# Attention with RMS-normed queries and keys, then a GELU feed-forward: in the second attention, batch 2's first loads are issued ahead of the transposes of batch 1's last heads

## The chip, the cores and the metric

The kernel runs on one core of a Trainium2 chip. That core has five engines with a queue of instructions each: TensorE (PE; its weight loads are shown apart, as PEld), VectorE (DVE), ScalarE (ACT), GpSimd (POOL) and SyncE (SP), which here only issues DMAs. Each engine works through its own queue in order and waits for the others by semaphores. Sixteen DMA engines move the data.

The metric is the device time of one execution in microseconds (us). The kernel before takes 390.83 us, the median of three executions (390.56 to 392.31).

## The reference

Eight batches of twelve heads, 448 tokens and 64 channels go through an attention whose queries and keys are normed by their root mean square and scaled by a gain per channel. The result, taken as 3584 tokens of 768 channels, goes through two matrix products with a GELU between them.

```python
def _attn_ref(q, k, v, g_q, g_k):            # q, k, v: (8, 12, 448, 64)
    def rmsnorm(x, g):
        rms = np.sqrt(np.mean(x * x, axis=-1, keepdims=True) + 1e-06)
        return x / rms * g
    q_n, k_n = (rmsnorm(q, g_q), rmsnorm(k, g_k))
    scores = 1.0 / np.sqrt(q.shape[-1]) * np.matmul(q_n, k_n.transpose(0, 1, 3, 2))
    scores = scores - np.max(scores, axis=-1, keepdims=True)
    attn = np.exp(scores)
    attn = attn / (np.sum(attn, axis=-1, keepdims=True) + 1e-09)
    return np.matmul(attn, v)

def _moe_ref(x, w_in, w_out):                # (3584, 768) x (768, 2048) x (2048, 768)
    h = x @ w_in
    c = np.float32(np.sqrt(2.0 / np.pi))
    g = 0.5 * h * (1.0 + np.tanh(c * (h + 0.044715 * h * h * h)))
    return g @ w_out
```

## The kernel before

**Tiling.** A batch's twelve heads are three chunks of four heads, numbered c = 0, 1, 2. For each chunk the queries and the keys are loaded as one tile each (`rawq`, `rawk`, 128 partitions x 896 numbers, 448 KB), squared, summed per row and channel group (`total`, L173), turned into reciprocal roots, multiplied by them (`normed`, L278, tiles `nrmq` and `nrmk`), and transposed so that the channels lie on the partitions (`qT`, `kT`). The gains of queries and keys are one product per channel, and it is multiplied into `kT` only: where the transpose is made by TensorE, that happens as VectorE copies the result out of PSUM (`put`, L305); where the transpose is made by a DMA (`dma_trans`, L319), VectorE multiplies the finished `kT` in place afterwards (`gain`, L325).

**Stages.** The program is a chain of stages, one batch after another: the attention of batch b + 1 is run together with the second matrix product of the feed-forward for tokens that are done (L495), and then comes the first matrix product for batch b + 1 (L537). The transposes, loads and sums for the next batches are strewn among them. What the change touches lies in the second attention, that of batch 1, for which `attention(1, ...)` is called with b = 0 in the loop of L918. In the trace of before it runs from 50.8 to 76.7 us.

**The order of the work is written out by hand.** `SECOND` (L577) holds two rows for this attention. The first is TensorE's: `u` is one unit of scores (four matmuls of L335; unit n belongs to chunk n // 7, so u14 is the first unit of chunk 2), `s` the row sums of a chunk and `x` its product with the values (both L387), and `8r` is eight steps of the second matrix product (four matmuls each). The second is VectorE's: `A`, `B`, `F`, `G` are additions of exponentials (L355 to L362), `T` (L397), `R` (L402) and `S` (L409) make the reciprocals of the row sums, and `M` (L422) writes the attention's output `xT`:

```python
"A0 L0 B0 F0 G0 L1 T0 R0 K0 S0 a0 M0 a1 T1 a2 R1 a3 S1 A2 a4 B2 a5 F2 M1 T2 R2 S2 M2"
```

`L0`, `L1`, `K0` and `a0` to `a5` are slots: what stands for them in the list `extra` is emitted at that place, and `"first"` in `extra` is emitted ahead of the whole attention. ScalarE makes one exponential (L343) for each unit and copies finished tiles of the second product out of PSUM (L518), from which SyncE stores them (L456).

**Loads and transposes in this stage.** `late_loads(b, c)` sets one number of each new raw tile to zero on VectorE (L142) and then issues the load on SyncE's queue; the load therefore waits for that place in VectorE's queue. `late_transposed(1, 2)` does the same for the transposes of chunk 2: VectorE sets one number of `qT` and one of `kT` (L908), and SyncE issues the two DMA transposes behind them (L319). `gpsimd_waits(x)` (L793) makes GpSimd copy one number of x, so that what follows on GpSimd waits for whoever writes x. In slot `K0` GpSimd is told to square batch 2's chunks 0 and 1 (L164): two whole tiles for chunk 0, four halves for chunk 1. VectorE sums them in `a0` to `a5`.

**Where things stand before the change.** The transposes of chunk 2 of batch 1 are emitted in step 6 of the first product for batch 0, before the attention begins. The loads of batch 2 come in `L0` (chunk 0), `L1` (chunk 1) and `a1` (chunk 2). The gain of chunk 2 comes in `K0`, behind the reciprocal R0, and GpSimd's squares wait for that gain.

Of the kernel before, what the change touches and what calls it, by code (L numbers as in the profile page):

```python
# [17 lines left out]
def kernel(  # L18
# [11 lines left out]
    nc = tc.nc  # L30
# [81 lines left out]
    kT = consts.tile([128, NCH, NT, 2, R], BF16)  # L112
# [5 lines left out]
    def load(b, c, n, parts=1, engs=(nc.sync,)):  # L118
        t = rawqk.tile([P, 2, NT, D], F32, tag=f"raw{n}", name=f"raw{n}")
        src = {"q": q, "k": k}[n]  # L120
        raws[n, b, c] = t
        m = 2 // parts
        return [
            lambda i=i: engs[i].dma_start(
                t[:, i * m:(i + 1) * m].rearrange("p a t d -> p a (t d)"),
                src[b, 4 * c + 2 * i * m:4 * c + 2 * (i + 1) * m].rearrange(
                    "(a r) (p t) d -> (r p) a (t d)", r=2, t=NT
                ),
            )
            for i in range(parts)  # L130
        ]
# [6 lines left out]
    def late_loads(b, c):  # L138

        for n in "qk":  # L140
            for go in load(b, c, n):
                nc.vector.memset(raws[n, b, c][:1, 0, 0, :1], 0.0)  # L142
                go()
# [140 lines left out]
    def qT_of(b):  # L284
        if b not in qT:
            qT[b] = qkp.tile([128, NCH, NT, 2, R], BF16, tag="qT", name="qT")
        return qT[b]
# [3 lines left out]
    def turn(b, c, n, ts=slice(0, NT)):  # L291

        if ts.start == 0 and ts.stop == NT:
            tps[n] = ps_m.tile([128, 1024], BF16, tag="mm", name="tp")
        for t in range(ts.start, ts.stop):
            nc.tensor.transpose(  # L296
                tps[n][:, t * 128:(t + 1) * 128],
                nrms[n, b, c][:, t].rearrange("p a d -> p (a d)"), ident,
            )

    def put(b, c, n, ts=slice(0, NT), eng=nc.vector):
        dst = (kT if n == "k" else qT_of(b))[:, c, ts]
        src = tps[n][:, :TR].rearrange("p (t r s) -> p t r s", r=2, s=R)[:, ts]
        if n == "k":
            nc.vector.tensor_scalar(dst, src, gcol[:, 0:1], None, op0=ALU.mult)  # L305
        elif eng is nc.scalar:
            nc.scalar.copy(dst, src)
        else:
            nc.vector.tensor_copy(dst, src)

    def trans(b, c, eng=nc.vector):
        for n in "qk":
            turn(b, c, n)
            put(b, c, n, eng=eng)
# [9 lines left out]
    def gain(b, c):  # L324
        nc.vector.tensor_scalar(kT[:, c], kT[:, c], gcol[:, 0:1], None, op0=ALU.mult)  # L325

    exs, ess, oas, scs = {}, {}, {}, {}
# [463 lines left out]
    def gpsimd_waits(x):  # L791

        nc.gpsimd.tensor_copy(mark, x)  # L793
# [106 lines left out]
    def transposed(b, c):  # L900
        for n in "qk":
            dma_trans(b, c, n)

    def late_transposed(b, c):

        for n in "qk":
            dst = kT if n == "k" else qT_of(b)
            nc.vector.memset(dst[:1, c, 0, 0, :1], 0.0)  # L908
        transposed(b, c)
# [4 lines left out]
    def normed_both(b, c, eng):  # L914
        for n in "qk":
            normed(b, c, n, eng)

    for b in range(B):  # L918
        m1, side, extra, ends = [], [], [], []
        if b == 0:  # L920

            m1 = [(0, lambda: total(1, 0, "k"),
                   lambda: total(1, 2, "q"), lambda: total(1, 2, "k"),
                   lambda: rsqrt_newton(1), lambda: normed_both(1, 2, nc.gpsimd),
                   lambda: normed(1, 0, "k", nc.gpsimd)),
                  (2, lambda: total(1, 1, "q"), lambda: total(1, 1, "k"),
                   lambda: normed(1, 0, "q", nc.vector), lambda: rsqrt_last(1),
                   lambda: normed_both(1, 1, nc.vector)),
                  (6, lambda: trans(1, 0, nc.scalar), lambda: late_transposed(1, 2)),
                  (7, lambda: trans(1, 1))]  # L930
            extra += [("L0", lambda: late_loads(2, 0)), ("L1", lambda: late_loads(2, 1)),
                      ("a1", lambda: late_loads(2, 2)),
                      ("K0", lambda: gain(1, 2))]

            for n in "qk":
                sqs[n, 2, 1] = [
                    nrmp.tile([P, NT, 2, D], BF16, tag=f"nrm{m}", name="sq")
                    .rearrange("p t a d -> p (t a d)").bitcast(F32)
                    .rearrange("p (a t d) -> p a t d", a=1, t=NT) for m in "qk"
                ]  # L940

            extra.append(("K0", lambda: gpsimd_waits(kT[:1, 2, 0, 0, :1])))
            at = 0
            for c in range(2):
                for n in "qk":
                    for hs in (slice(0, 1), slice(1, 2)) if c else (both,):
                        extra += [
                            ("K0", lambda c=c, n=n, hs=hs: square(2, c, n, nc.gpsimd, hs)),
                            (f"a{at}", lambda c=c, n=n, hs=hs: total(2, c, n, hs))]
                        at += 1  # L950
        elif b + 1 < B:

            m1.append((0, lambda: gpsimd_waits(ess[b, NCH - 1][:1, 0, 0, :1])))
            for c in range(NCH):
                if b == 1 and c + 1 == NCH:
                    m1 += [(0, lambda: total(2, 2, "q")), (0, lambda: total(2, 2, "k")),
                           (0, lambda: rsqrt_last(2))]
                m1 += [(0, lambda c=c: normed_both(b + 1, c, nc.gpsimd)),
                       (4 * c + 4, lambda c=c: transposed(b + 1, c))]
            m1 += [(9, lambda: gain(b + 1, 0)), (14, lambda: gain(b + 1, 1))]  # L960
        if 0 < b and b + 2 < B:
            m1 += [(4, lambda: loads(b + 2, 1)), (8, lambda: loads(b + 2, 2))]
            for c, at in ((0, 4), (1, 9)):
                for i, (n, a) in enumerate((n, a) for n in "qk" for a in range(2)):
                    m1.append((at + i, lambda c=c, n=n, a=a: squared(b + 2, c, n, a)))
                m1 += [(at + 2, lambda c=c: total(b + 2, c, "q")),
                       (at + 4, lambda c=c: total(b + 2, c, "k"))]
            for n in "qk":
                m1.append((13, lambda n=n: square(b + 2, 2, n, nc.gpsimd)))
                extra.append(("first", lambda n=n: total(b + 2, 2, n)))  # L970
        if 0 < b and b + 1 < B:
            extra.append(("first", lambda: gain(b + 1, 2)))
        m1 = plan(*m1)
        for f in range(nf // 2 if b == 0 else nf):
            i, part = f // 4 * 2, f % 4
            if b == 0:
                if f == 2:
                    mm1(0, 5)
                    square(1, 1, "k", nc.scalar)
                elif f > 2:  # L980
                    mm1_pair(f)
            elif f == 1:
                mm1_turn(b, 0, 1, late)
                mm1_turn(b, 1, 1, late)
                mm1_turn(b, 0, 0, late, end=True)
            elif f == 3:
                mm1_turn(b, 1, 0, late, end=True)
            elif part == 1:
                mm1_turn(b, i, 0, range(HP), begin=True)
                mm1_turn(b, i + 1, 0, range(HP), begin=True)  # L990
                mm1_turn(b, i, 1, range(HP), end=True)
            elif part == 3:
                mm1_turn(b, i + 1, 1, range(HP), end=True)
            for fn in m1.get(f, ()):
                fn()
        if b + 1 == B:
            final(b)
            break
        nc.scalar.preload_act_table_set(EXP_SET)
        if b + 2 < B:  # L1000
            ends.append(lambda: rsqrt(b + 2, slice(0, NCH if b else NCH - 1)))
            side += [(0 if b else 11, lambda: load_v(b + 2, 0, HP))]
            if b + 3 < B:
                side.append((3, lambda: loads(b + 3, 0)) if b else (14, lambda: late_loads(3, 0)))
        if b == 0:
            start.close()
            ps_x = ctx.enter_context(
                tc.tile_pool(name="ps_x", bufs=1, space=bass.MemoryType.PSUM))
            for i in (2, 3):
                rounds.append(ps_x.tile([128, 2, 512], F32, tag=f"t{i}", name=f"t{i}"))  # L1010
            late_on.append(b)
        attention(b + 1, plan(*side), plan(*extra), ends)
# [30 lines left out]
```

## Time and profile before

| | |
|---|---|
| median of three executions | 390.83 us (390.56 to 392.31) |
| the profiled execution | 391.29 us, of which the span of instructions is 389.5 us |
| mean granted TensorE clock | 0.998 |
| TensorE busy | 381.4 us, 98% of the span |
| ScalarE busy | 278.7 us, 72% |
| VectorE busy | 236.6 us, 61% |
| GpSimd busy | 125.2 us, 32% |

All times of a trace are in us from the start of the span. In a row of the timeline stand the start, the duration, the engine, the line of the kernel, the operation, what it writes and reads, shapes and the number of instructions; in brackets the idle time ahead of it and what ended it. In a row of a table by stages stand the stretch, its length, and for each engine its busy time and in brackets its instructions, then the granted clock, the mean busy share of the DMA engines and what they moved in GB/s. For a DMA, the "time to landing" runs from the start of its issue on the queue to the last part of its data.

### The profile page before, as it was taken

To read this page: it belongs to the slowest core of one execution; us is meant where nothing else is said; L and a number is where in the kernel's file an instruction comes from. 1 tells how busy PE (TensorE), PEld (TensorE's weight loads), DVE (VectorE), ACT (ScalarE), POOL (GpSimd) and SP (SyncE) were. 2 spreads that over 40 slices of the span, in tenths; PEclk is the share of its full clock that TensorE was granted. 3 is DMA by queue.
4 is the path that set the end of the run, shared out by engine and by line. 5 is a ranking of instruction groups with operands and counts; after the bars stand their busy time and mean duration, and the time that the engine had idled before them with its cause. 6 is when DMAs were issued, how large, how long until landed. Compare 5 with 4: busy or idle time off the path is not lost.

```text
span 389.5 us, 17541 instructions
## 1 busy us (share of the span) xinstructions
PE 381.4 (98%) x8060; PEld 293.4 (75%) x8060; DVE 236.6 (61%) x367; ACT 278.7 (72%) x353; POOL 125.2 (32%) x107
## 2 busy tenths in 40 slices
PE   8799999999999999999999999999999999999996
PEld 5465567877888788877888778877888778887664
DVE  5899938976597259835589256953598204980010
ACT  6995589767994689757996589946897449944300
POOL 4996505484005540083102740064400900000000
PEclk9999999999999999999999999999999999999999
DMA  8999997999614993379822995159622621120033
GB/s 276 315 224 210 210 163 250 247 266 256 114 44 94 223 222 71 84 133 221 185 69 65 197 239 108 44 104 253 112 74 54 123 46 42 44 65 4 2 82 81
DMA packets 64414, 54.68 MB, mean 140 GB/s; under 512 B 37588, under 2 KB 59988, under 8 KB 64340
## 3 DMA queue, kind: packets, MB, share of 16 engines
q1 hardware_dynamic: 53904, 41.33, 45.3%
q0 software_dynamic: 10128, 11.80, 18.5%
q8 instruction: 63, 1.03, 1.1%
q10 hardware_dynamic: 308, 0.43, 0.4%
q14 instruction: 11, 0.09, 0.1%
HBM read 45.61 MB, written 11.01 MB: 145 GB/s over the span
## 4 chain that ended last, share of the span: by engine, by line
PE 92%; ACT 4%; DMA 2%; POOL 1%; SPq 0%; DVE 0%; issue 0%; DVEq 0%
PE t L537 33%; PE t L495 32%; PE t L387 9%; PE t L335 7%; PE t L463 5%; PE t L556 4%; ACT ex L343 4%; DMA rawq<-in_q_dram 2%; POOL g L164 1%; PE h L436 1%; PE tp L296 0%; PE o L387 0%; SPq L745 0%; PE os L387 0%; DVE ss L173 0%; ACT lg L198 0%
## 5 line engine op out<-in xcount | busy, mean ns | idle before, releaser
L343 ACT ACTIVATE ex<-t,shift 128x896 bf16<-128x896 f32 x168 | 156.2, 1016 | 1.9 <-PE t L335 1.6
L495 PE MATMUL t<-wout,g 64*64 64x384 bf16 (+1 forms) x3456 | 150.6, 305 | 0.0
L537 PE MATMUL t<-xT,win 64*64 64x448 bf16 x2688 | 128.6, 349 | 0.0
L495 PEld LDWEIGHTS <-g 64*64 64x64 bf16 x3456 | 112.6, 107 | 19.5
L537 PEld LDWEIGHTS <-win 64*64 64x64 bf16 x2688 | 96.1, 107 | 31.0
L543 ACT ACTIVATE g<-t 128x896 bf16<-128x896 f32 x56 | 50.5, 915 | 57.1 <-PE t L537 57.1
L173 DVE TENSOR_REDUCE ss<-sq 128x14 f32<-128x896 f32 (+3 forms) x45 | 44.6, 997 | 52.9 <-ACT sq L162 49.1
L335 PE MATMUL t<-qT,kT 64*64 64x448 bf16 x672 | 58.1, 351 | 2.3 <-ACT ex L343 0.8
L355 DVE TENSOR_TENSOR es<-ex 128x1792 bf16<-128x1792 bf16 x20 | 21.1, 1058 | 32.4 <-ACT ex L343 32.4
L278 POOL TENSOR_TENSOR nrmq<-rawq,rinv 128x896 bf16<-128x896 f32 (+1 forms) x21 | 34.8, 1659 | 17.6 <-ACT rinv L205 9.9
L793 POOL COPY mark<-es 1x1 bf16<-1x1 bf16 x6 | 1.1, 177 | 117.1 <-DVE es L362 112.9
L278 POOL TENSOR_TENSOR nrmk<-rawk,rinv 128x896 bf16<-128x896 f32 x20 | 33.6, 1679 | 0.0
L387 PE MATMUL t<-ex,vb 64*64 64x448 bf16 x588 | 31.9, 350 | 0.0
L335 PEld LDWEIGHTS <-kT 64*64 64x64 bf16 x672 | 25.4, 106 | 8.3 <-DVE kT L305 2.2
L397 DVE STREAM_TRANSPOSE st<-t 128x448 f32<-128x448 f32 x42 | 24.7, 627 | 9.1 <-PE t L387 9.1
L387 PEld LDWEIGHTS <-vb 64*64 64x64 bf16 x672 | 23.5, 107 | 7.1 <-issue 0.8
L409 DVE STREAM_TRANSPOSE rb<-rc 128x896 f32<-128x896 f32 (+1 forms) x25 | 26.7, 1067 | 0.3
L701 DVE COPY osb<-t 128x384 f32<-128x384 f32 (+1 forms) x4 | 2.0, 508 | 35.2 <-PE t L463 35.2
L422 DVE TENSOR_TENSOR xT<-t,rb 128x896 bf16<-128x896 f32 x21 | 22.8, 1085 | 0.8
L513 ACT COPY osb<-t 128x768 f32<-128x768 f32 (+1 forms) x18 | 12.6, 701 | 14.0 <-PE t L495 14.0
L164 POOL TENSOR_TENSOR sq<-rawq 128x896 f32<-128x896 f32 (+1 forms) x9 | 13.6, 1511 | 27.9 <-DVE ss L173 21.6
L358 DVE TENSOR_TENSOR es<-es,ex 128x1792 bf16<-128x1792 bf16 x20 | 21.3, 1063 | 0.7 <-ACT ex L343 0.7
(103 smaller groups left out, 315.4 us busy)
## 6 DMA issues: line engine op xcount, KB each, us to landing
rawq<-in_q_dram SPq DMA_DIRECT2D x23, 448.0 KB, 5.1
rawk<-in_k_dram SPq DMA_DIRECT2D x23, 448.0 KB, 5.8
out_dram<-osb SPq DMA_DIRECT2D x42, 192.0 KB, 2.7
vb<-in_v_dram POOLq DMA_DIRECT2D x6, 672.0 KB, 7.4
win<-in_moe_w_in_dram POOLq DMA_DIRECT2D x8, 384.0 KB, 10.5
wout<-in_moe_w_out_dram POOLq DMA_DIRECT2D x3, 768.0 KB, 17.3
out_dram<-osb SPq DMA_DIRECT2D x24, 96.0 KB, 3.5
vb<-in_v_dram POOLq DMA_DIRECT2D x2, 448.0 KB, 15.7
```

The lines of the kernel that those rows point to most:

```text
L173: nc.vector.reduce_sum(sss[b][:, seat(b, c), "qk".index(n), hs, ts], squares(b, c, n, hs, ts), axis=AX.X)
L278: eng.tensor_mul(nrms[n, b, c][:, ts].rearrange("p t a d -> p a t d"), raws[n, b, c][:, :, ts], root[:, :, ts].to_broadcast([P, 2, m, D]),)
L335: nc.tensor.matmul(sc[r * R:(r + 1) * R, a, :S], kT[rs, c, t, r], qT[b][rs, c, :, r], start=True, stop=True,)
L343: nc.scalar.activation(exs[b, c][:, t], scs.pop((b, c, t))[:, :, :S], AF.Exp, scale=scale, bias=shift)
L358: nc.vector.tensor_add(es, es, ex[:, 4:6])
L387: nc.tensor.matmul(o[r][a * D:(a + 1) * D], vb[b % 2][rs, 2 * c + a, i] if what else ones[rs], es[i][rs, a], start=(i == 0), stop=(i == n ...
L397: nc.vector.transpose(st[:, r].rearrange("p a b -> p (a b)"), o[r])
L409: nc.vector.transpose(oas["rb"][:, rs].rearrange("p r s -> p (r s)"), rc.to_broadcast([128, (rs.stop - rs.start) * m, 32]),)
L422: nc.vector.tensor_mul(xT[b][:, 2 * c:2 * c + 2], oas["o", c, 1][:, :, :S], oas["rb"])
L495: mm = nc.tensor.matmul(o[a * R:(a + 1) * R, bank, :hi - lo], g[rs, f, at:at + R], wout[rs, f, lo:hi], start=(n == 0), stop=(n == len(step ...
L537: mm = nc.tensor.matmul(h[a * R:(a + 1) * R, j, :S], win[rs, c, at:at + R], xT[b][rs, c], start=begin and c == cs[0], stop=end and c == cs ...
L543: nc.scalar.activation(g[:, 2 * i:2 * i + 2, (b % 2) * S:(b % 2 + 1) * S], h[:, :, :S], AF.Gelu_apprx_tanh,)
```

## The change

Four entries of the plan of the second attention are moved or replaced:

- `late_transposed(1, 2)`, the two DMA transposes of batch 1's chunk 2 with their two VectorE memsets, goes from step 6 of the first product to slot `L0`, behind VectorE's first addition A0.
- `late_loads(2, 0)`, the first two loads of batch 2 with their memsets, goes from `L0` to `"first"`, ahead of the attention. On SyncE's queue these loads now stand ahead of the two transposes.
- `gain(1, 2)`, VectorE's multiplication of the transposed keys by the gain, goes from `K0` to `a1`, behind M0 and behind the memsets of the loads of batch 2's chunk 2.
- GpSimd's squares of batch 2 wait for the reciprocals of R0 (`oas["rc"]`) and no more for the gain.

```diff
@@ -926,11 +926,11 @@
                   (2, lambda: total(1, 1, "q"), lambda: total(1, 1, "k"),
                    lambda: normed(1, 0, "q", nc.vector), lambda: rsqrt_last(1),
                    lambda: normed_both(1, 1, nc.vector)),
-                  (6, lambda: trans(1, 0, nc.scalar), lambda: late_transposed(1, 2)),
+                  (6, lambda: trans(1, 0, nc.scalar)),
                   (7, lambda: trans(1, 1))]
-            extra += [("L0", lambda: late_loads(2, 0)), ("L1", lambda: late_loads(2, 1)),
-                      ("a1", lambda: late_loads(2, 2)),
-                      ("K0", lambda: gain(1, 2))]
+            extra += [("first", lambda: late_loads(2, 0)), ("L0", lambda: late_transposed(1, 2)),
+                      ("L1", lambda: late_loads(2, 1)), ("a1", lambda: late_loads(2, 2)),
+                      ("a1", lambda: gain(1, 2))]
@@ -939,7 +939,7 @@
-            extra.append(("K0", lambda: gpsimd_waits(kT[:1, 2, 0, 0, :1])))
+            extra.append(("K0", lambda: gpsimd_waits(oas["rc"][:1, :1])))
```

## The prediction

> **What bounds the kernel now.** I read the page first: TensorE's share, and the chain that ended last.
>
> ```profile
> PE 381.4 (98%) x8060; PEld 293.4 (75%) x8060; DVE 236.6 (61%) x367; ACT 278.7 (72%) x353; POOL 125.2 (32%) x107
> PE 92%; ACT 4%; DMA 2%; POOL 1%; SPq 0%; DVE 0%; issue 0%; DVEq 0%
> ```
>
> The second row is the chain: TensorE's own work sets the end. Next the busy times by stage: the second attention up to its unit u14, the rest of it, and all that follows to the last product.
>
> ```profile
> 50.84:65.52 14.68, 14.68 (x345) 10.54 (x348) 7.94 (x16) 14.65 (x18) 2.67 (x3) 1.00 1.12 214
> 65.52:76.71 11.19, 11.19 (x260) 8.89 (x253) 11.19 (x21) 9.16 (x15) 5.54 (x8) 1.00 0.88 221
> 76.71:346.77 270.06, 270.06 (x6462) 218.70 (x6457) 171.61 (x235) 208.25 (x257) 81.87 (x56) 1.00 0.62 129
> ```
>
> In each stretch TensorE (the first engine after the length) is busy for the whole length. Two things follow. The change can't win much, since no TensorE stall of any size is there to be removed. And a stall that it puts into TensorE's queue has no idle time behind it that could take it up. (Busy matmuls are modelled and may hide waits of some hundredths, so "much" means a few tenths here.) In the second stretch VectorE, the third figure, is busy for all 11.19 us too, so it has no room for extra work there either.
>
> So the question is which of TensorE's waits moves. One candidate: u14, the first unit that reads the chunk 2 keys whose transpose and gain are moved. The timelines of TensorE and its weight loads, and VectorE's, around it:
>
> ```profile
> 64.03 1.52 PE L387 MATMUL t<-ex,vb 64*64 64x448 bf16 x28
> 65.36 0.14 PEld L335 LDWEIGHTS <-kT 64*64 64x64 bf16 x4
> 65.52 0.39 PE L335 MATMUL t<-qT,kT 64*64 64x448 bf16 x4
> ```
>
> ```profile
> 62.19 0.33 DVE L402 RECIPROCAL rc<-st 128x28 f32<-128x28 f32 x1
> 62.43 0.35 DVE L325 TENSOR_SCALAR kT<-kT,gcols 128x896 bf16<-128x896 bf16 x1
> 62.70 1.10 DVE L409 STREAM_TRANSPOSE rb<-rc 128x896 f32<-128x896 f32 x1
> 64.69 1.09 DVE L173 TENSOR_REDUCE ss<-sq 128x14 f32<-128x896 f32 x1 [0.88 <-POOL sq L164]
> 65.69 1.08 DVE L422 TENSOR_TENSOR xT<-t,rb 128x896 bf16<-128x896 f32 x1
> 66.71 1.07 DVE L173 TENSOR_REDUCE ss<-sq 128x14 f32<-128x896 f32 x1
> 67.72 0.64 DVE L397 STREAM_TRANSPOSE st<-t 128x448 f32<-128x448 f32 x1
> ```
>
> Before, the gain (L325) is over at 62.78, and u14's weights load at 65.36 without a wait for it. M0 (L422) starts at 65.69, when x0, the product with the values, has ended (64.03 + 1.52 = 65.55).
>
> **The change part by part.**
>
> *The gain goes behind M0.* This is the term that decides. VectorE's queue now reads S0, a0, M0, the memsets, gain, sum, T1. M0 stays where x0's end puts it, and the next instruction starts at 66.71; the memsets of the loads cost nothing there, as they already stand between M0 and the sum that starts at 66.71. So the gain runs from 66.71. How long? The rows of all other gains give 443 to 875 ns, the one of this stage 353:
>
> ```profile
> L325 DVE TENSOR_SCALAR kT<-kT,gcols x18: 443/445/875, 88.9 to 314.7; 128x896 bf16<-128x896 bf16 x18
> 59.72 0.63 DVE L362 TENSOR_TENSOR es<-es,ex 128x896 bf16<-128x896 bf16 x1
> 60.49 0.36 PE L387 MATMUL t<-es,ones 64*64 64x448 bf16 x4
> ```
>
> I take 0.40, between the 0.35 and the median 0.445: it ends at 67.11. From the end of a VectorE result to the first matmul that waits for it the last two rows give 60.49 - 60.35 = 0.14. u14 thus starts at 67.25 in place of 65.52, **1.73 us later**. Behind u14 in TensorE's queue stands everything else: s1, u15 to u20, the second product, the whole rest of the program.
>
> What is late next? T1 needs s1, which needs u14's place in the queue: T1 comes 1.73 late by TensorE, but it was held back by the sum until 67.72 where s1 had ended by 67.4 or so, hence 1.45 late. From T1 on VectorE runs without a gap to F2, for which s2 waits:
>
> ```profile
> 68.87 0.57 DVE L173 TENSOR_REDUCE ss<-sq 128x7 f32<-128x448 f32 x1
> 74.12 0.60 DVE L360 TENSOR_TENSOR es<-es 128x896 bf16<-128x896 bf16 x1
> 74.81 0.39 PE L387 MATMUL t<-es,ones 64*64 64x448 bf16 x4
> 66.51 6.62 ACT L343 ACTIVATE ex<-t,shift 128x896 bf16<-128x896 f32 x7
> ```
>
> F2 ends at 74.72 + 1.45 = 76.17, and s2, at 74.81 + 1.73 = 76.54, finds it done. The seven exponentials of chunk 2 shift with their units and stay ahead of the additions. So no second stall here: +1.73.
>
> *The gain leaves the place ahead of S0.* S0 starts 0.27 earlier (62.70 - 62.43), and nothing gains by it: M0 waits for x0, not for S0. 0.
>
> *GpSimd waits for the reciprocals.* They are there at 62.52, the gain at 62.78. The squares start some 0.26 earlier than these rows:
>
> ```profile
> 62.85 0.18 POOL L793 COPY mark<-kT 1x1 bf16<-1x1 bf16 x1 [17.52 <-DVE kT L325]
> 66.26 0.92 POOL L164 TENSOR_TENSOR sq<-rawq 128x448 f32<-128x448 f32 x1
> ```
>
> The first sum, a0, comes 0.26 earlier into the gap before M0: 0. But the gain and the squares may now run side by side, which the old wait excluded (rivals).
>
> *The loads of batch 2's chunk 0 go ahead.* Their memsets come behind VectorE's last copy before the attention, some 5.4 us before 57.1:
>
> ```profile
> 51.03 0.68 DVE L305 TENSOR_SCALAR kT<-tp,gcols 128x896 bf16<-128x896 bf16 x1
> 56.07 1.09 DVE L355 TENSOR_TENSOR es<-ex 128x1792 bf16<-128x1792 bf16 x1 [4.36 <-ACT ex L343]
> 57.10 0.06 DVE L142 MEMSET rawq<- 1x1 f32 x1
> 49.17 1.32 SPq L319 DMA_TRANSPOSE qT<-nrmq  x1
> 50.60 3.82 SPq L319 DMA_TRANSPOSE kT<-nrmk  x1
> 57.21 0.38 SPq L124 DMA_DIRECT2D rawq<-in_q_dram  x1
> 58.23 3.32 SPq L456 DMA_DIRECT2D out_dram<-osb  x4
> 61.64 0.55 SPq L124 DMA_DIRECT2D rawq<-in_q_dram  x1
> 62.28 1.91 SPq L124 DMA_DIRECT2D rawk<-in_k_dram  x1
> ```
>
> Their squares wait for the reciprocals at 62.52 anyway. They now share the DMA engines with the weights and values that GpSimd has queued, where the transposes did so before. The rate of all transfers from 48 us on, in slices of 0.6 us:
>
> ```profile
> GB/s 213 207 207 212 222 187 202 202 197 194 207 166 133 90 74 52 54 230 333 343 376 388 375 272 153 202 357 173 182 340 260 39 0 128 284 357 137 127 214 349
> ```
>
> It falls from 55 us on (the 13th slice) and rises only with the loads of 57.21: the rest of GpSimd's transfers is small by 56. The values are first read by x0 at 64.03, so loads that mix with them from 52 on have 8 us to spare. 0.
>
> *The transposes go behind A0.* Their memsets take the place of the loads', at 57.10. On SyncE's queue the queries' transpose starts at 57.2 and the keys' about 1.4 later (the two rows of before start 1.4 apart), at 58.6. Time to landing of the keys' transpose, in all later stages (min/median/max), and of the one here before, when the engines were full:
>
> ```profile
> DMA to landing us min/median/max: 2.9/4.3/7.4
> DMA to landing us min/median/max: 8.9/8.9/8.9
> ```
>
> So from 58.6 on they land at 62.9 by the median, at 66.0 by the longest of the later ones, at 67.5 by the crowded one; I take the median, since the crowd is gone by then. The gain comes at 66.71: covered but for the last. If not covered, each us costs a us.
>
> *Stores and chunk 1's loads slide on SyncE.* Behind the transposes stand four stores (3.32) and then chunk 1's loads. If the keys' transpose takes 1.3 to issue like the queries', SyncE is through with it at 59.9, with the stores at 63.3, and issues the query tile then in place of 61.64; if it takes the 3.82 of before, at 65.8. The square of its first half must be done when a2 starts, at 68.87 + 1.45 = 70.3, so the tile must land by 69.3. Time to landing of this very load before, and the median of all such loads:
>
> ```profile
> DMA to landing us min/median/max: 4.4/4.4/4.4
> rawq<-in_q_dram SPq DMA_DIRECT2D x23, 448.0 KB, 5.1
> ```
>
> From 63.3 it lands at 67.7 or 68.4: covered by 0.9 at least.
>
> **Sum:** 391.29 + 1.73 = 393.0 for an execution like the profiled one. The median of the three runs lies 0.46 below that execution, so **392.6 us** is the forecast, 0.44% slower.
>
> **The rivals.**
>
> (a) *The gain is held up by a square on GpSimd.* Later in the program gain and square do meet:
>
> ```profile
> 138.92 0.88 DVE L325 TENSOR_SCALAR kT<-kT,gcols 128x896 bf16<-128x896 bf16 x1
> 137.86 1.68 POOL L164 TENSOR_TENSOR sq<-rawq 128x896 f32<-128x896 f32 x1 [6.27 <-DMA rawq<-in_q_dram]
> ```
>
> The gain took 0.88 where others take 0.445, and ended 0.26 after the square beside it. The Trainium skill, page "SBUF — State Buffer", section "SBUF: two separate sides", states that VectorE in a two-port mode and GpSimd take a shared pair of ports in turn, each for a whole instruction; this pair of rows agrees. Here: if chunk 1's query tile lands between 65.8 and 66.7, a half square of 0.92 is running at 66.71, and the gain ends 0.3 behind it, at 67.3 to 67.9, so 0.2 to 0.8 is added: 392.8 to 393.4. Against it: by the landing above the tile comes at 67.7, and then the gain is first.
>
> (b) *Late transposes.* By 8.9 to landing the keys are there at 67.5, the gain ends at 67.9, and u14 is 2.5 late: 393.4. For it: that figure is this stage's own. Against: the row of rates, by which the crowd of then is gone.
>
> (c) *Late second loads.* If the keys' transpose holds SyncE for the 3.82 of before, chunk 1's query tile, issued at 65.8, lands at 70.2 to 70.9; a2 waits for 0.9 to 1.6, F2 with it, and what exceeds F2's spare 0.37 s2 waits too: 0.5 to 1.2 more, 393.1 to 393.8. For it: such an issue is in the trace. Against: it fell into the crowded time.
>
> (d) *Not slower.* Were the gain over before 65.2 (the weights load at 65.36 less 0.14), u14 wouldn't wait, and the transposes would only have to land by then, which 62.9 does. That needs the gain ahead of M0 on VectorE, in the 0.88 us gap at 63.8. The written order puts it behind M0, and M0 can't move before x0's end at 65.55; so this holds only if TensorE doesn't in fact wait for VectorE there. Time: 390.5 to 390.9, a win of at most the few tenths hidden in busy matmuls.
>
> **How the numbers follow.** 0.5% of 390.83 is 1.95 us, about what a measurement of this kernel can tell from no change; the three runs alone span 1.75. My forecast lies 0.2 under that bound, so its chance of 0.50 falls on both sides of it, 0.26 same and 0.24 slower. (a) 0.18, nearly all slower; (b) 0.09, slower; (c) 0.10, slower; (d) 0.07, of which 0.05 same and 0.02 faster; the remaining 0.06, unforeseen, in equal parts same and slower. Together: faster 0.02, same 0.34, slower 0.64. The range goes from 391.7 (a gain of 0.35, and half the stall taken up by waits that busy matmuls hide) to 394.0, the end of (c) and a little for (b) and (c) together.
>
> **What would show it.** In the trace after: the gain right behind M0 at about 66.7; a TensorE gap of 1.5 to 1.8 us before the unit behind x0, ended by VectorE's `kT` L325; no gap at s2; from there all stages later by the same amount. Wrong would be: the gap ended by a DMA (b), a gain of 0.6 or more with a square beside it (a), a second gap at s2 (c), or no gap (d).

## The result: a little slower, by one wait before u14

The kernel after takes 392.75 us, the median of 17 executions (391.76 to 394.65); 17 executions of the kernel before, made beside them, have a median of 391.72 us (390.56 to 392.31). The ratio is 1.0031, with a 95% interval from 1.0016 to 1.0046: slower by 0.6 to 1.8 us, which is less than 0.5%.

The profiled execution after took 392.03 us, with a span of 390.2, only 0.7 longer than before. That difference hides two of opposite sign. The tables by stages of both kernels show them; the first two of the three stretches end where the second attention's first matmul (L495) and the next first product's first matmul (L537) start. First before, then after:

```profile
0.00:50.77 50.77, 46.29 (x484) 28.18 (x484) 41.53 (x93) 36.64 (x53) 35.07 (x42) 1.00 1.07 246
50.77:76.52 25.75, 25.75 (x595) 19.35 (x597) 19.01 (x36) 23.69 (x32) 8.03 (x9) 1.00 1.02 217
76.52:389.50 312.98, 309.35 (x6989) 245.82 (x6980) 176.02 (x240) 218.40 (x270) 82.06 (x56) 1.00 0.55 117
```

```profile
0.00:49.86 49.86, 46.52 (x484) 28.48 (x484) 41.60 (x91) 36.53 (x53) 35.03 (x42) 1.00 1.08 248
49.86:77.16 27.30, 25.84 (x596) 17.71 (x597) 19.65 (x38) 23.79 (x32) 8.09 (x10) 1.00 0.95 234
77.16:390.20 313.04, 309.39 (x6988) 241.66 (x6980) 176.78 (x240) 218.28 (x270) 81.92 (x56) 1.00 0.55 115
```

The first figure after the stretch is its length, the next TensorE's busy time. The second attention took 27.30 us in place of 25.75, **1.55 longer**, and TensorE is idle in it for 1.46 where it was never idle before. Everything behind it took the same (313.04 and 312.98). The time up to the attention was 0.91 shorter. That is no gain of the change: it differs from execution to execution (49.85 to 51.18 us among the traces of kernels with the same code up to there), and the chain of before goes there through a first load of 6.26 us, that of after through one of 3.19. So the stage is to be compared by its own length.

The timelines after, around u14, of TensorE, VectorE, GpSimd and SyncE:

```profile
63.11 1.52 PE L387 MATMUL t<-ex,vb 64*64 64x448 bf16 x28
64.43 0.36 PE L495 MATMUL t<-wout,g 64*64 64x384 bf16 x4
66.26 0.38 PE L335 MATMUL t<-qT,kT 64*64 64x448 bf16 x4 [1.47 <-DVE kT L325]
75.45 0.36 PE L387 MATMUL t<-es,ones 64*64 64x448 bf16 x4
```

```profile
61.64 1.11 DVE L409 STREAM_TRANSPOSE rb<-rc 128x896 f32<-128x896 f32 x1
63.51 1.09 DVE L173 TENSOR_REDUCE ss<-sq 128x14 f32<-128x896 f32 x1 [0.76 <-POOL sq L164]
64.73 1.09 DVE L422 TENSOR_TENSOR xT<-t,rb 128x896 bf16<-128x896 f32 x1
65.76 0.45 DVE L325 TENSOR_SCALAR kT<-kT,gcols 128x896 bf16<-128x896 bf16 x1
66.12 1.08 DVE L173 TENSOR_REDUCE ss<-sq 128x14 f32<-128x896 f32 x1
69.19 0.58 DVE L173 TENSOR_REDUCE ss<-sq 128x7 f32<-128x448 f32 x1
74.44 0.61 DVE L360 TENSOR_TENSOR es<-es 128x896 bf16<-128x896 bf16 x1
```

```profile
66.63 1.82 POOL L164 TENSOR_TENSOR sq<-rawq 128x448 f32<-128x448 f32 x2 [1.51 <-DMA rawq<-in_q_dram]
```

```profile
59.20 3.55 SPq L456 DMA_DIRECT2D out_dram<-osb  x4
62.84 0.54 SPq L124 DMA_DIRECT2D rawq<-in_q_dram  x1
```

u14 was due 0.16 behind the four matmuls of 64.43, as before (65.36, 65.52), that is at 64.59. It starts at 66.26, 1.67 late, and its wait ends with VectorE's gain (65.76 + 0.45 = 66.21), which stands behind M0 (64.73). VectorE idles for 0.76 ahead of the sum at 63.51, in a place where the gain could have run. The sum at 69.19 is a2, the first of chunk 1, and needs the first of the two half squares that start at 66.63. F2 (74.44) is over at 75.05, 0.40 before s2 (75.45), where before it ended only 0.09 ahead of it.

### The profile page after: what moved, and what is told of

Read it like the earlier page. It is cut to its first block, busy times and chain, and to the rows that moved or that the text cites. A ratio compares the mean times of both kernels' runs of the same rounds, so it can differ in the third digit from the quotient of the medians.

```text
span 390.2 us, 17541 instructions
## 1 busy us (share of the span) xinstructions
PE 381.8 (98%) x8060; PEld 287.9 (74%) x8060; DVE 238.0 (61%) x367; ACT 278.6 (71%) x353; POOL 125.0 (32%) x107
## 3 DMA queue, kind: packets, MB, share of 16 engines
q8 instruction: 63, 1.03, 1.1%
## 4 chain that ended last, share of the span: by engine, by line
PE 92%; ACT 5%; DVE 1%; DMA 1%; issue 0%; POOL 0%; DVEq 0%
PE t L537 33%; PE t L495 32%; PE t L387 9%; PE t L335 7%; PE t L463 5%; ACT ex L343 4%; PE t L556 4%; DMA rawq<-in_q_dram 1%; PE h L436 1%; PE tp L296 1%; PE o L387 0%; DVE ss L173 0%; DVE xT L422 0%; POOL nrmq L278 0%; PE os L387 0%
## 5 line engine op out<-in xcount | busy, mean ns | idle before, releaser
L495 PE MATMUL t<-wout,g 64*64 64x384 bf16 (+1 forms) x3456 | 150.7, 305 | 0.0
L537 PE MATMUL t<-xT,win 64*64 64x448 bf16 x2688 | 128.5, 349 | 0.0
L495 PEld LDWEIGHTS <-g 64*64 64x64 bf16 x3456 | 110.1, 107 | 22.5 <-issue 0.2
L537 PEld LDWEIGHTS <-win 64*64 64x64 bf16 x2688 | 94.0, 107 | 33.1
```

The costliest lines, as they stand in the source:

```text
L495: mm = nc.tensor.matmul(o[a * R:(a + 1) * R, bank, :hi - lo], g[rs, f, at:at + R], wout[rs, f, lo:hi], start=(n == 0), stop=(n == len(step ...
L537: mm = nc.tensor.matmul(h[a * R:(a + 1) * R, j, :S], win[rs, c, at:at + R], xT[b][rs, c], start=begin and c == cs[0], stop=end and c == cs ...
```

## Experiments: where the gain stands, and what the moved transfers do by themselves

Two theories first. **The gain's place**: the whole cost is that u14 waits for a gain that stands behind M0. **The moved transfers**: the loads and transposes in their new order cost the time, by SyncE's queue or by full DMA engines. Beside them stood the forecast's rival that a square on GpSimd holds up the gain. The first four kernels were timed together on one chip, with 30 executions of the kernel before (median 391.23 us). "Stage" is the length of the second attention, taken as above.

**The gain ahead of M0, all else as after.**

```diff
-                      ("a1", lambda: gain(1, 2))]
+                      ("a0", lambda: gain(1, 2))]
```

> The kernel after, with the gain of chunk 2 in slot a0, ahead of M0 in VectorE's queue, and all else as after. Theory 1 (the whole cost is that unit u14 waits for a gain that stands behind M0): no TensorE gap before u14, from the start of the second product to the start of the next first product 25.75 us as before (after: 27.30), and a time ratio to before of 1.000. Theory 2 (the cost comes from the moved loads and transposes, by SyncE's queue or full DMA engines): the stage stays at 27 us or more, ratio 1.003.

Measured: 390.96 us median (390.55 to 392.59), ratio 0.9992 (0.9976 to 1.0008). The table by stages, then TensorE's, VectorE's and GpSimd's rows:

```profile
50.38:76.22 25.84, 25.84 (x594) 19.09 (x596) 19.94 (x38) 23.78 (x32) 8.33 (x10) 1.00 0.89 230
```

```profile
64.96 0.36 PE L495 MATMUL t<-wout,g 64*64 64x384 bf16 x4
65.12 0.39 PE L335 MATMUL t<-qT,kT 64*64 64x448 bf16 x4
```

```profile
63.19 1.06 DVE L325 TENSOR_SCALAR kT<-kT,gcols 128x896 bf16<-128x896 bf16 x1
65.26 1.09 DVE L422 TENSOR_TENSOR xT<-t,rb 128x896 bf16<-128x896 f32 x1
68.44 0.57 DVE L173 TENSOR_REDUCE ss<-sq 128x7 f32<-128x448 f32 x1
```

```profile
62.33 1.67 POOL L164 TENSOR_TENSOR sq<-rawq 128x896 f32<-128x896 f32 x1
67.30 1.83 POOL L164 TENSOR_TENSOR sq<-rawq 128x448 f32<-128x448 f32 x2 [1.51 <-DMA rawq<-in_q_dram]
```

u14 (65.12) follows the four matmuls ahead of it by 0.16 again, TensorE is busy throughout, and the stage is 0.09 longer than before, not 1.55. Everything else of the change is still there, GpSimd's new wait too. That speaks for the gain's place. The gain itself took 1.06 in place of 0.45 beside a square (62.33 to 64.00) and ended at 64.25, but here the delay fell into VectorE's gap.

**Only the gain moved.** Loads and transposes stay where they were before. GpSimd's wait goes to the reciprocals with the gain, as in the change.

```diff
-                      ("K0", lambda: gain(1, 2))]
+                      ("a1", lambda: gain(1, 2))]
...
-            extra.append(("K0", lambda: gpsimd_waits(kT[:1, 2, 0, 0, :1])))
+            extra.append(("K0", lambda: gpsimd_waits(oas["rc"][:1, :1])))
```

> The kernel before, with only the gain moved to a1 and GpSimd's wait set on the reciprocals; loads and transposes stay where they were. Theory 1: the TensorE gap before u14 is there, 1.4 to 1.6 us, and the stage takes 27.3 us, ratio 1.003 to 1.0045. Theory 2: no gap, ratio 1.000. Theory 3 (a square on GpSimd holds up a gain that meets it): in this order chunk 1's query tile lands near 66.0, its first half square of 0.92 runs when the gain comes at 66.7, and the gain takes 0.6 to 0.8 in place of 0.45, which adds 0.2 to 0.4 to the gap; if squares and gain don't disturb each other, the gain takes 0.35 to 0.45.

Measured: 392.91 us (392.24 to 394.36), ratio 1.0044 (1.0026 to 1.0062). The table by stages, TensorE's row of u14, then VectorE's and GpSimd's rows beside it:

```profile
49.93:77.77 27.84, 25.89 (x596) 17.79 (x597) 20.12 (x36) 23.81 (x32) 8.24 (x10) 1.00 1.02 227
```

```profile
66.87 0.38 PE L335 MATMUL t<-qT,kT 64*64 64x448 bf16 x4 [1.95 <-DVE kT L325]
```

```profile
65.88 0.93 DVE L325 TENSOR_SCALAR kT<-kT,gcols 128x896 bf16<-128x896 bf16 x1
```

```profile
65.63 0.93 POOL L164 TENSOR_TENSOR sq<-rawq 128x448 f32<-128x448 f32 x1 [0.45 <-DMA rawq<-in_q_dram]
```

The gain's place alone makes the whole cost, and more than it: the stage is 27.84 us long, 2.09 longer than before. The 0.54 beyond the kernel after are the rival with the square: in this order chunk 1's query tile is there early, its half square starts at 65.63, and the gain of 65.88 ends at 66.81, 0.25 after it, having taken 0.93 in place of 0.45. In the kernel after the tile lands too late for that: its half square starts at 66.63, with the gain over at 66.21.

**The gain back behind R0, the transposes still behind A0.**

```diff
-                      ("a1", lambda: gain(1, 2))]
+                      ("K0", lambda: gain(1, 2))]
```

> The kernel after, with the gain back in slot K0, behind R0 and ahead of S0; the transposes stay behind VectorE's first addition and GpSimd's wait stays on the reciprocals. Theory 1: VectorE waits some tenths at most for the keys' transpose (issued at 57.9, landing 2.9 to 4.3 later, so by 62.2, against R0's end at 61.6), no TensorE gap before u14, stage 25.75 to 25.9 us, ratio 1.000. Theory 2: stage 27 us or more, ratio 1.003, whatever the gain's place.

Measured: 391.38 us (390.62 to 393.08), ratio 0.9999 (0.9983 to 1.0015). No gap at u14, as the first theory has it. But the stage of the profiled execution took 26.86 us, 1.11 longer than before, which that theory doesn't have. The table by stages, and the rows of SyncE, GpSimd, VectorE and TensorE that show why:

```profile
49.88:76.74 26.86, 25.95 (x594) 19.05 (x596) 19.45 (x38) 24.80 (x32) 9.26 (x10) 1.00 0.91 232
```

```profile
59.50 4.03 SPq L456 DMA_DIRECT2D out_dram<-osb  x4
63.62 0.54 SPq L124 DMA_DIRECT2D rawq<-in_q_dram  x1
```

```profile
67.82 1.82 POOL L164 TENSOR_TENSOR sq<-rawq 128x448 f32<-128x448 f32 x2 [2.61 <-DMA rawq<-in_q_dram]
```

```profile
68.78 0.62 DVE L173 TENSOR_REDUCE ss<-sq 128x7 f32<-128x448 f32 x1 [0.78 <-POOL sq L164]
74.35 0.61 DVE L360 TENSOR_TENSOR es<-es 128x896 bf16<-128x896 bf16 x1
```

```profile
75.01 0.38 PE L387 MATMUL t<-es,ones 64*64 64x448 bf16 x4 [0.91 <-ACT osb L518]
```

The four stores behind the transposes held SyncE until 63.53. Chunk 1's query tile was issued at 63.62 (before: 61.64, with an attention that began 0.89 later), its square began at 67.82, the sum a2 waited 0.78 for it, and F2 was over at 74.96, 0.05 ahead of s2. Counted from the matmuls ahead of it as in the trace of before, s2 came 1.11 late, the whole excess of the stage. (The profile names ScalarE's copy as the end of that wait. But in the trace of before, s2 began at 74.81, ahead of that copy, which began at 75.06; so by the times it was F2.) The ratio of all executions leaves room for 0.15% at most, 0.6 us, so this wait of about one us does not seem to occur in full in most of them.

In the first experiment the same loads had the same place in SyncE's queue, and a2 did not wait: they were issued 13.24 after the attention's start in place of 13.74, and a2 (68.44) found its half square over by some 0.2 us. The second wait was close there too.

**The gain one place further back.** It stands behind the sum that follows it in `a1`.

```diff
-                      ("a1", lambda: gain(1, 2))]
...
                         at += 1
+            extra.append(("a1", lambda: gain(1, 2)))
```

> The kernel after, with the gain one more place back in VectorE's queue: behind the sum of 1.08 us that follows it in slot a1. Theory 1: the gap before u14 grows by one sum, from 1.47 to about 2.5 us, the stage to 28.3 us, and the time by 2.6 us over before, ratio 1.0065. Theory 2: the gap does not follow the gain's place one to one, ratio 1.003 as after.

Measured: 393.92 us (392.91 to 396.69), ratio 1.0066 (1.0040 to 1.0092). The table by stages, then VectorE, GpSimd, TensorE:

```profile
51.18:79.97 28.79, 25.84 (x596) 17.72 (x597) 20.13 (x38) 23.79 (x32) 8.24 (x10) 1.00 0.93 228
```

```profile
67.08 1.07 DVE L173 TENSOR_REDUCE ss<-sq 128x14 f32<-128x896 f32 x1
68.08 0.93 DVE L325 TENSOR_SCALAR kT<-kT,gcols 128x896 bf16<-128x896 bf16 x1
```

```profile
67.83 1.97 POOL L164 TENSOR_TENSOR sq<-rawq 128x448 f32<-128x448 f32 x2 [1.39 <-DMA rawq<-in_q_dram]
```

```profile
69.07 0.38 PE L335 MATMUL t<-qT,kT 64*64 64x448 bf16 x4 [2.95 <-DVE rawk L142]
```

The stage is 28.79 us long, and the gap follows the gain: 2.95 in place of 1.47. (The wait is put down to a memset behind the gain; the gain ended at 69.01, u14 began at 69.07.) It grew by 1.48, not by the 1.0 expected, since the later gain met the half square of 67.83 and took 0.93 in place of 0.45.

**The second cost by itself.** The kernel of the third experiment showed a wait that the first theory doesn't explain. So chunk 1's loads were issued ahead of the stores:

```diff
-                      ("L1", lambda: late_loads(2, 1)), ("a1", lambda: late_loads(2, 2)),
+                      ("L0", lambda: late_loads(2, 1)), ("a1", lambda: late_loads(2, 2)),
                       ("K0", lambda: gain(1, 2))]
```

> The kernel of the third experiment (the change with the gain in K0), and with the loads of batch 2's chunk 1 issued right behind the transposes, ahead of the four stores. In the third experiment the stage took 26.85 us in place of 25.74, with VectorE waiting 0.78 us for a square of chunk 1. Theory A (the moved transposes and the stores push chunk 1's loads back on SyncE, its sums come late, and s2 waits for them): the query tile is issued near 59.2 in place of 63.6, VectorE's wait and TensorE's gap of 0.91 us before s2 are gone, and the stage takes 25.8 us. Theory B (the gap before s2 comes from something else, such as ScalarE's copy or crowded DMA engines): the gap stays, and the stage takes 26.5 us or more.

Measured: 391.17 us (390.38 to 391.70) against 391.29 for 23 executions of the kernel before on the same chip, ratio 0.9992 (0.9974 to 1.0010). The stage, SyncE and GpSimd:

```profile
49.85:75.59 25.74, 25.74 (x594) 19.36 (x596) 19.17 (x38) 23.68 (x32) 8.11 (x9) 1.00 0.90 215
```

```profile
59.19 0.54 SPq L124 DMA_DIRECT2D rawq<-in_q_dram  x1
59.82 0.45 SPq L124 DMA_DIRECT2D rawk<-in_k_dram  x1
60.36 3.93 SPq L456 DMA_DIRECT2D out_dram<-osb  x4
```

```profile
65.14 1.82 POOL L164 TENSOR_TENSOR sq<-rawq 128x448 f32<-128x448 f32 x2
```

With the tile issued at 59.19, its squares follow chunk 0's without a wait, and the gap before s2 is gone: 25.74 us, the length of before. So in the traces the wait at s2 goes with the late loads. The times of all executions do not tell the two kernels apart: the intervals of their ratios overlap, and neither differs from before. The changed order, with the gain and chunk 1's loads put right, shows no cost, and no gain either.

**Only the first loads moved.**

```diff
-            extra += [("L0", lambda: late_loads(2, 0)), ("L1", lambda: late_loads(2, 1)),
+            extra += [("first", lambda: late_loads(2, 0)), ("L1", lambda: late_loads(2, 1)),
```

> The kernel before, with only the first loads of batch 2 moved ahead of the attention; transposes, gain and GpSimd's wait stay. If the early loads are worth nothing by themselves, as TensorE is busy throughout: stage 25.7 to 25.8 us, no TensorE gap, ratio 1.000. If they relieve a later crowd: stage or rest of the program shorter by some tenths, ratio 0.999. If they crowd the weights and values on the DMA engines: a gap before u14 or earlier, ratio above 1.000.

Measured: 391.57 us (390.39 to 392.99), ratio 1.0009 (0.9994 to 1.0025), on the chip of the last experiment.

```profile
49.87:75.61 25.74, 25.74 (x595) 19.31 (x597) 19.00 (x36) 23.68 (x32) 8.03 (x9) 1.00 1.02 230
```

The loads are issued earlier, though not as early as in the change, since SyncE still has the transposes ahead of them: at 53.58, 3.71 after the attention's start, where before it was 6.44 and in the change 1.02. The early loads are worth nothing by themselves: TensorE has no wait in this stage that they could shorten, and the rest of the program takes 312.99 us (before: 312.98).

## Why the prediction was right

The time (392.75) lies in the range, and the direction and the place are as forecast. Step by step:

- *What bounds the kernel.* That TensorE has no idle time to take up a stall holds: the 1.55 us of the stage come back nowhere in the 313 us behind it.
- *The gain behind M0.* This was the deciding term, 1.73 us. u14 was 1.67 late. The gain took 0.445, not 0.40; from its end to u14 there were 0.05, not 0.14, because the matmul of 60.49 that the 0.14 was read from was held by TensorE's own unit of 60.30 and not by VectorE. The two errors partly cancel, which is luck. M0 came where it was forecast, but not quite for the reason given: in the trace of before it (65.69) followed the sum of 64.69 without a gap, and only after, where GpSimd's earlier start had moved that sum forward, was it by the times the end of x0 (64.63) that set M0 (64.73). Of the 1.67 the stage shows 1.55: some 0.1 came back between u14 and s1 (0.31 from start to start before, 0.21 after), where the forecast had none.
- *The base.* 392.6 was reached from a median of three executions, 390.83. The median of 17 is 391.72. The cost was forecast as 1.73 and measured between the medians as 1.03 (0.6 to 1.8 by the interval). So part of the closeness of 392.6 to 392.75 is luck: a base 0.9 too low and a cost that, by the medians, was too high. The stage's 1.55 is the cleaner measure, and it lies inside the interval.
- *No second stall at s2.* Right for the kernel after, and with about the spare that was worked out: F2 was over 0.40 ahead of s2, where 0.37 was forecast. Both came less late than forecast, F2 by 1.23 in place of 1.45 and s2 by 1.55 in place of 1.73, counted from the attention's start.
- *Transposes behind A0.* The keys' transpose was issued 1.44 behind the queries', as forecast, and never held the gain: in the third experiment, where the gain stood earliest, it starts at 61.54 right behind R0, 3.4 us after the keys' transpose was issued at 58.18. Rival (b), late transposes, did not occur in any trace.
- *Stores and chunk 1's loads.* The loads were issued at 62.84, 12.98 after the attention's start, where 63.3 less 50.77, or 12.5, was forecast, and the tile landed 3.7 later. It was covered, by 1.6: the first half square, 0.93 long, was over at 67.56, and a2 came at 69.19. Of that, 1.2 is u14's own delay, which moved the sums back; 0.4 would have been left without it, as 0.2 was in the first experiment. In the third nothing was left. That is the wait of rival (c), but not from the cause that the forecast gave: the keys' transpose took 1.23 to issue, not 3.82. The queries' transpose (1.61 in place of 1.32) and the stores (4.03 in place of 3.55) took longer, and the tile took 4.1 to land.
- *Rival (a), the square.* It did not occur in the kernel after, by 0.42 us (gain over at 66.21, half square from 66.63), and did in the three experiments where a square was under way when the gain came: it cost u14 half a us in the second and fourth, and nothing in the first.
- *Rival (d), no wait.* Excluded by the gap itself.
- *The chances.* 0.64 was given to slower by over 0.5%, and the time came out below that, 0.31% slower. Nearly half of the forecast's own case was put past the bound, and the rivals (a) to (c), all of which add to the cost, had 0.37 together. The waits of (a) and (c) exist, as the experiments show, but in the kernel after each missed its moment; (b) was not seen.

## What to carry to other kernels

An instruction that another engine waits for is as late as whatever stands ahead of it in its own queue. Before one is moved, look for the instruction ahead of its new place that waits for a third engine, here M0 for x0, and put the piece that others wait for into a gap in front of it. And where the engine that bounds the program has no idle time, transfers that come earlier win nothing, while a wait put into its queue is paid nearly in full (1.55 of 1.67 us here). The length of the changed stage shows that better than the time of a few executions.

## What the runs showed of the hardware

By its end times VectorE's gain, a bf16 copy with a factor, waits for a square on GpSimd that is under way: it ended 0.25, 0.25 and 0.25 us after the square in the first, second and fourth experiment (64.25 after 64.00, 66.81 after 66.56, 69.01 after 68.76; the ends from the start of the square and its duration, 0.93 for the half in the fourth), however early it had been issued, so that its duration was 1.06, 0.93 and 0.93 in place of 0.35 to 0.45. That it waits was on record with the prediction; that the tail is the same each time was not expected. The Trainium skill, page "SBUF — State Buffer", section "Who interferes with whom", states that between GpSimd and a VectorE instruction in a two-port mode, whichever issues first holds the shared ports for its whole instruction. The three ends agree with it: each time the square had started first.

SyncE's issue of the four stores varies with nothing changed in them or ahead of them in its queue for this stage: 3.55 us after, and 3.81, 4.03 and 3.27 in the first, third and fourth experiment. What stands behind stores in its queue can't be timed here to better than 0.8 us.
